# A second store buffer for one output projection, and a projection that starts three units later

## The chip, the cores and the metric

The kernel runs on one core of one Trainium2 chip. The metric is the time of one execution on the device, in microseconds (us); smaller is better. All runs quoted here are of the same state (called fast: none is over 1.5% above the fastest run of its kernel), and each kernel was timed several times beside the kernel before on the same chip.

## The reference, cut to what matters

(Condensed.) The program computes two attention blocks and all their gradients in one launch. Block A is a linear attention and takes about the first fifth of the time (its last result is copied at 217 us of 1179); the change doesn't touch it. Block B is attention with 16 query heads that share one key and one value head (2048 tokens, head size 28, padded to 32):

```python
q = (x @ wq).reshape(B, S, H, Dh).transpose(0, 2, 1, 3)
k = x @ wk
v = x @ wv
scores = einsum("bhqd,bkd->bhqk", q, k) * Dh ** -0.5
p = softmax(scores)
o = einsum("bhqk,bkd->bhqd", p, v)
return o.transpose(0, 2, 1, 3).reshape(B, S, H * Dh) @ wo     # the output projection of B
# and the gradients of this for x, wq, wk, wv, wo, from grad_out
```

The gradient of `o` begins with grad_out @ wo^T. The kernel calls that product the do-projection.

## The kernel before

The core of block B is a software pipeline of 512 units. One unit takes two 128-row key tiles for one pair of heads and 256 queries. TensorE (PE) computes scores and dP (the gradient of `p`), ScalarE (ACT) takes the exponential into `eT`, VectorE (DVE) and GpSimd (POOL) multiply to `dsT`, and PE accumulates o, dq, dk and dv. For dv the kernel needs the exponentials transposed. SyncE (SP) issues one DMA transpose for every two units, and dv uses the four transposes of a block (8 units) together, 13 units after the last one's data is ready:

```python
if u % 2 == 1:
    en = pn_.tile([P, 16, P], BF16, name="eN")                     # 12 buffers
    nc.sync.dma_start_transpose(en[:, :, :], et[...])              # 512 KB
    eN[u // 2] = en
...
if (b := due(u, 20)) is not None:
    dv_mm(b, 0)                                                    # reads eN of block b
```

Once in 64 units SyncE also loads `qX`, the queries in the layout that dk wants:

```python
if u == 14 or u % 64 == 32 and u < 448:
    qx = pq_.tile([P, 4, 2, 512], BF16, name="qX")
    for a in range(4):
        for B in range(4):                                         # 16 DMAs of 64 KB
            r0 = qc * 256 + 64 * B
            nc.sync.dma_start(qx[32 * a:32 * a + 32, B, :, :],
                              qn_d[r0:r0 + 64, :].rearrange("(j s) c -> j s c", s=2))
```

The output projection is done for two token tiles in every 64 units, four units apart, and VectorE casts each result into the one buffer, from which SyncE stores it:

```python
def out_store(u, ps):                                              # at u % 64 in (20, 24), u > 64
    i = 2 * (u // 64 - 1) + (u % 64 == 24)
    ot = flat(R3)[:, 5120:5120 + D]
    nc.vector.tensor_copy(out=ot, in_=ps[:, 0:D])                  # L636
    nc.sync.dma_start(out0[i * P:(i + 1) * P, D:2 * D], ot)        # L637
```

The do-projection is done during the first units ("the fill"), when the later stages of the pipeline have no work yet: tile `v` in unit `v + 1`, so in units 1 to 16.

## Time and profile before

| | before |
|---|---|
| time, median of 3 runs | 1177.76 us (1172.9 to 1179.81) |
| PE busy / VectorE busy / ScalarE busy | 91% / 77% / 74% |
| DMA queue 1 (SyncE's DMAs, the transposes among them), share of 16 engines | 94.3% |
| core of B, from the end of unit 1's exponentials to the end of unit 511's | 255.7 to 1097.3 us |

The page's groups of instructions (busy us, mean ns of one, then the idle time of the engine just before and what ended most of it) show VectorE idle for 44.6 us before only 16 casts, and PE idle before the score matmuls for the same cast:

```profile
L591 PE MATMUL sps<-R,R 32*128 32x256 bf16 x2048 | 248.4, 282 | 50.9 <-DVE R L636 30.9
L636 DVE CAST R<-sps 128x448 bf16<-128x448 f32 x16 | 9.9, 620 | 44.6 <-DMA out_dram<-R 42.9
```

The view of waits (who waited for whom: us in total, times, longest) has the same two, and, far down, the one wait of PE for a transpose:

```profile
DVE R L636 <- DMA out_dram<-R: 42.9, 8, 9.6
PE sps L591 <- DVE R L636: 30.9, 7, 8.9
...
PE dv_acc L591 <- DMA eN<-eT: 0.8, 1, 0.8
```

Eight pairs of casts make eight waits: the second cast of a pair may not overwrite the buffer before the first one's store has landed. The last of the eight, 7.4 us, comes after the core; 35.5 us fall in it. The timeline of VectorE (start, duration, what, idle before) at the first pair:

```profile
394.00 0.61 DVE L636 CAST R<-sps 128x448 bf16<-128x448 f32 x1
...
399.62 0.69 DVE L831 TENSOR_TENSOR dsT<-dps,eT 128x512 bf16<-128x512 f32 x1 [0.16 <-PE dps L591]
409.88 0.62 DVE L636 CAST R<-sps 128x448 bf16<-128x448 f32 x1 [9.58 <-DMA out_dram<-R]
```

Why does a store of 112 KB take from 394.6 to 409.9 us? The timeline of SyncE's queue (runs of equal DMAs are merged; x9 is nine of them) answers:

```profile
381.84 25.41 SPq L857 DMA_TRANSPOSE eN<-eT  x9
407.34 0.81 SPq L637 DMA_DIRECT2D out_dram<-R  x1
408.25 4.84 SPq L857 DMA_TRANSPOSE eN<-eT  x2
413.18 0.56 SPq L637 DMA_DIRECT2D out_dram<-R  x1
413.85 11.57 SPq L857 DMA_TRANSPOSE eN<-eT  x4
425.55 9.59 SPq L806 DMA_DIRECT2D qX<-qn_d  x16
```

SyncE issues in program order and leaves no gap, and it is behind: the cast ends at 394.6, its store goes out at 407.34. The store itself landed some 2.5 us later. I call SyncE's delay the lag: the time from the end of the exponentials that a transpose reads to that transpose's issue. It stood at 11 to 13 us here.

The view by windows (busy us and number of instructions of each engine in 25 us, then granted TensorE clock, DMA share, GB/s) shows the price. The first and second line have the stall; the third is an undisturbed stretch, in which two units take 3.04 us:

```profile
core 0: us, PE busy (x) PEld busy (x) DVE busy (x) ACT busy (x) POOL busy (x), PEclk, DMA share, GB/s
380.00:405.00 25.00, 20.69 (x362) 9.28 (x359) 19.47 (x36) 20.36 (x41) 17.60 (x20) 1.00 1.19 195
405.00:430.00 25.00, 18.88 (x314) 7.83 (x317) 18.23 (x35) 17.20 (x34) 13.69 (x16) 0.80 0.98 180
430.00:455.00 25.00, 23.81 (x438) 10.41 (x431) 23.95 (x46) 24.80 (x51) 20.70 (x24) 1.00 0.97 171
```

The granted clock (the share of TensorE's full clock that the trace records as let through) falls to 0.80 in the stretch around the stall. In the trace's record of it, it is half for 10.2 us from 406.5 us, and for 3.4 or 6.8 us at every later stall in the core. The Trainium skill, "TensorE: Matmul & The Clock Gate", section "Part 1: The HAM clock gate", has the clock halved after an idle window of about 3.4 us. The first stall fits, with PE idle for 8.9 us. But at three of the seven stalls PE's timeline has a gap of only 2.7 to 3.1 us, and the clock was halved all the same, so here a shorter idle was enough (the ends of matmuls are modelled, so such a gap is exact to some tenths of a us).

### The profile page before, as it was taken

The numbers are of one execution on the slowest core, as the hardware profiler recorded it, in microseconds if no ns is written. First come the engines' busy times: TensorE is split into PE (matmuls) and PEld (weight loads), VectorE is DVE, ScalarE is ACT, GpSimd is POOL, SyncE is SP. The second block draws the span as 40 slices with busy tenths as digits, with TensorE's granted clock in tenths as the row PEclk, the third lists the DMA queues.
The fourth block names the chain that finished last, engine by engine and source line by source line (L and its number), as shares of the span: only waits on it lengthen the run. The fifth ranks groups of instructions, "written<-read, shape, count | busy, mean of one in ns | idle before, by whom it ended". The sixth has DMA issues, their size and how long they took to land.

```text
span 1179.1 us, 38599 instructions
## 1 busy us (share of the span) xinstructions
PE 1072.2 (91%) x15379; PEld 487.1 (41%) x15388; DVE 902.6 (77%) x1733; ACT 877.4 (74%) x1724; POOL 696.6 (59%) x835
## 2 busy tenths in 40 slices
PE   7999997988999699989989997999899899989898
PEld 4555543433344244434434443444344344434344
DVE  7886400335899699989989997998899799989922
ACT  3453112356899699989989997999899799989511
POOL 9000141002778578868868885887688688768800
PEclk9999998988799899999999998999899999989999
DMA  9779798049999989999998999999899999999962
GB/s 259 126 130 185 146 172 194 24 84 214 191 166 191 188 167 185 181 189 177 188 189 160 182 185 188 169 185 183 168 183 189 187 168 180 194 177 174 244 144 75
DMA packets 684437, 202.92 MB, mean 172 GB/s; under 512 B 651232, under 2 KB 679392, under 8 KB 684256
## 3 DMA queue, kind: packets, MB, share of 16 engines
q1 hardware_dynamic: 673664, 190.26, 94.3%
q10 hardware_dynamic: 9312, 6.65, 2.0%
q0 software_dynamic: 1280, 3.55, 1.2%
q8 instruction: 120, 1.97, 0.7%
q14 instruction: 61, 0.50, 0.1%
HBM read 22.83 MB, written 15.03 MB: 32 GB/s over the span
## 4 chain that ended last, share of the span: by engine, by line
PE 59%; DVE 21%; ACT 9%; issue 4%; DMA 4%; SPq 1%; POOL 1%; ACTq 0%; DVEq 0%; POOLq 0%
PE dk_acc L591 16%; PE agen L79 10%; DVE dsT L831 8%; PE sps L591 7%; PE dps L591 6%; PE oq L591 6%; DVE dsx L894 4%; ACT eT L854 4%; PE aacc L79 4%; PE sps L79 4%; PE dv_acc L591 3%; ACT eT L826 2%; PE dps L79 2%; DVE R L840 2%; DMA out_dram<-R 2%
## 5 line engine op out<-in xcount | busy, mean ns | idle before, releaser
L834 POOL TENSOR_TENSOR dsT<-cp,eT 128x512 bf16<-128x512 bf16 x512 | 591.4, 1155 | 201.0 <-ACT cp L833 199.0
L831 DVE TENSOR_TENSOR dsT<-dps,eT 128x512 bf16<-128x512 f32 x512 | 345.8, 675 | 37.9 <-PE dps L591 29.0
L826 ACT ACTIVATE eT<-sps 128x512 bf16<-128x512 f32 x512 | 306.6, 599 | 73.3 <-PE dps L591 51.1
L894 DVE STREAM_TRANSPOSE dsx<-dsT 128x512 f32<-128x512 f32 x512 | 357.8, 699 | 2.0
L591 PEld LDWEIGHTS <-R 32*128 32x128 bf16 (+1 forms) x8192 | 200.0, 94 | 350.7 <-issue 302.9
L833 ACT ACTIVATE cp<-dps 128x512 bf16<-128x512 f32 x512 | 304.2, 594 | 14.6 <-PE dps L591 13.5
L854 ACT ACTIVATE eT<-sps 128x512 bf16<-128x512 f32 x512 | 310.6, 607 | 0.0
L591 PE MATMUL sps<-R,R 32*128 32x256 bf16 x2048 | 248.4, 282 | 50.9 <-DVE R L636 30.9
L591 PE MATMUL dk_acc<-dsx,qX 32*32 32x512 bf16 x4096 | 275.9, 385 | 0.0
L591 PE MATMUL dps<-doT,R 32*128 32x256 bf16 x2048 | 262.5, 277 | 9.5 <-DVE dsT L831 6.9
L591 PE MATMUL oq<-eT,R 128*32 128x256 bf16 x2048 | 162.2, 282 | 0.0
L591 PE MATMUL oq<-dsT,R 128*32 128x256 bf16 x2048 | 161.9, 281 | 0.1
L591 PEld LDWEIGHTS <-qX 32*32 32x32 bf16 x4096 | 81.2, 90 | 119.3 <-issue 61.3
L591 PE MATMUL dv_acc<-eN,don 128*32 128x512 bf16 x1024 | 80.7, 385 | 0.8 <-DMA eN<-eT 0.8
L521 DVE TENSOR_TENSOR osb<-R 32x512 bf16<-32x512 bf16 x4 | 1.7, 413 | 78.2 <-ACT R L518 78.2
L380 POOL MEMSET ga<- 64x448 bf16 x2 | 0.9, 469 | 90.6 <-PE agen L337 71.3
L79 PEld LDWEIGHTS <-R 128*128 128x128 bf16 (+1 forms) x416 | 34.4, 100 | 36.5 <-issue 12.6
L636 DVE CAST R<-sps 128x448 bf16<-128x448 f32 x16 | 9.9, 620 | 44.6 <-DMA out_dram<-R 42.9
L553 POOL MEMSET R<- 128x16 bf16 x1 | 0.2, 173 | 70.1 <-DVE R L552 70.1
L719 POOL TENSOR_TENSOR don<-R,rl 128x128 bf16<-128x128 bf16 x64 | 25.8, 403 | 21.2 <-DVE rl L711 21.2
L79 PE MATMUL agen<-R,R 128*128 128x448 bf16 x128 | 30.4, 369 | 3.2 <-DVE pk L227 1.9
L486 ACT ACTIVATE osb<-agen 128x448 bf16<-128x448 f32 x16 | 8.7, 542 | 28.9 <-DMA R<-xa 13.7
(203 smaller groups left out, 982.3 us busy)
## 6 DMA issues: line engine op xcount, KB each, us to landing
qX<-qn_d SPq DMA_DIRECT2D x128, 64.0 KB
out_dram<-osb ACTq DMA_DIRECT2D x44, 112.0 KB
eN<-eT SPq DMA_TRANSPOSE x256
qn_d<-dsx SPq DMA_DIRECT2D x1, 2048.0 KB
on_d<-onat SPq DMA_DIRECT2D x8, 256.0 KB
xa<-in_A_x_dram SPq DMA_DIRECT2D x8, 224.0 KB
ga<-in_grad_out_dram SPq DMA_DIRECT2D x4, 448.0 KB
xa<-in_grad_out_dram POOLq DMA_DIRECT2D x4, 448.0 KB, 5.0
```

Of the source, the lines that this page charges most:

```text
L79: nc.tensor.matmul(out_ap, lhsT=lhsT, rhs=rhs, start=start, stop=stop, tile_position=(0, 0))
L486: nc.scalar.activation(out=ot[:], in_=ps[:, :], func=ACT.Copy)
L591: nc.tensor.matmul(out, lhsT=lhsT, rhs=rhs, start=start, stop=stop, tile_position=pos, skip_group_check=True)
L636: nc.vector.tensor_copy(out=ot, in_=ps[:, 0:D])
L719: nc.gpsimd.tensor_tensor(out=dn[:], in0=dnv, in1=r_[:].to_broadcast([P, 2, 2, 32]), op=ALU.mult)
L826: nc.scalar.activation(out=et[:, u % 2, 0, :], in_=sp[0][:, :], func=ACT.Exp, scale=scale)
L831: nc.vector.tensor_tensor(out=dst[:, 0, :], in0=dp[0][:, :], in1=ew[:, w % 2, 0, :], op=ALU.mult)
L833: nc.scalar.activation(out=cp[:, :], in_=dp[1][:, :], func=ACT.Copy)
L834: nc.gpsimd.tensor_tensor(out=dst[:, 1, :], in0=cp[:, :], in1=ew[:, w % 2, 1, :], op=ALU.mult)
L840: nc.vector.tensor_scalar(out=qT_B[g][64 * hp:64 * hp + 64, qc * 256:(qc + 1) * 256], in0=oq[64:128, 0:256], scalar1=scale, scalar2=None, ...
L854: nc.scalar.activation(out=et[:, u % 2, 1, :], in_=sp[1][:, :], func=ACT.Exp, scale=scale)
L894: nc.vector.transpose(out=dsx[b][:, tp, :, :, :].rearrange("p h t c -> p (h t c)").bitcast(F32), in_=dsT[y][:, :, :].rearrange("p h c -> p ...
```

## The change

Its intent: give the second store of a pair its own buffer, so that no cast waits for a store; and start the do-projection three units later, two tiles in some units, so that it is out of the very first units and done before unit 16, from which the dP matmuls use the same two PSUM banks.

```diff
         def out_store(u, ps):
             i = 2 * (u // 64 - 1) + (u % 64 == 24)
-            ot = flat(R3)[:, 5120:5120 + D]
+            ot = pp_.tile([P, D], BF16, name="ot", bufs=1) if i % 2 else flat(R3)[:, 5120:5120 + D]
@@
-                v = u - 1
                 y = u - 18

-                if 0 <= v < NS:
-                    ps = DB[v % 2]
-                    for c in range(4):
-                        mm(ps[:, :], gbT[:, v, c, :], woTp[:, c, :], start=(c == 0), stop=(c == 3))
-                    nc.vector.tensor_copy(out=do_nat[:, v, :], in_=ps[:, :])
+                for i in range(NS):
+                    if u == 4 + 3 * i // 4:
+                        ps = DB[i % 2]
+                        for c in range(4):
+                            mm(ps[:, :], gbT[:, i, c, :], woTp[:, c, :], start=(c == 0), stop=(c == 3))
+                        nc.vector.tensor_copy(out=do_nat[:, i, :], in_=ps[:, :])
```

No work is added or removed, and the order of SyncE's DMAs is the same in both kernels.

## The prediction

> **What bounds the kernel now.** The page shows PE 91% busy, VectorE 77%, DMA queue 1 at 94.3% of 16 engines. In undisturbed stretches of the core (timeline, 440 to 480 us) two units take 3.04 us. Once in 64 units this pace breaks. The groups table has the cast of the output projection (L636) idle 42.9 us before it, 8 times, released by the store `out_dram<-R`; the waits view has PE waiting 30.9 us, 7 times, for that cast. Timeline of the first pair: the cast at 394.0 is stored only at 407.34, because SyncE issues in order and is some 13 us behind with the `eN<-eT` transposes; the second cast waits 9.58 us for that one buffer. The granted clock drops in the same stretches (windows view: 0.80 to 0.93 instead of 1.00). A semaphore wait happens on the issuing sequencer and not in the DMA engine (Trainium skill, "DMA: Bandwidth & Descriptors", section "Anatomy of one DMA — SWDGE (gpsimd) path"); the trace agrees: SyncE's rows follow one another without a gap for tens of us.
>
> **What the change does.** No work is added or removed: 16 casts (0.62 us), 16 stores, 64 matmuls of do-projection stay; SyncE's order is the same. (a) The second store of a pair gets its own buffer, so both casts have 64 units for their store: the 42.9 us of VectorE idle and the 30.9 us of PE wait go. (b) The do-projection runs in units 4 to 15 instead of 1 to 16: it leaves the half-clock start of the core (clock 0.5, 252.9 to 259.7 us; 0.53 us per matmul there, 0.26 later) and no longer shares the DB banks with unit 16. Worth 2 to 5 us of the fill.
>
> **How much is on the critical path.** Less than it looks, because the DMA stream is the next limit and almost equal. Whenever SyncE is behind, one `eN` transpose costs 2.82 to 2.88 us from issue to issue (26 of them from 334.3 to 410.5, less the other DMAs). One period of 64 units then needs 32 x 2.85 for `eN`, about 9.4 for `qX`, 2 for `on_d` and `oTq`, 1.6 for the stores: about 104 us at worst, 102 at best, against 104.3 measured (413.85 to 1039.47 over 6) and 97.3 plus two longer units for the engines. SyncE's own gaps between 400 and 1098 add to only 23 us, and its transposes get dearer when it never rests. So the stall mostly moves: PE will wait for `eN` at L591 (dv_acc), 2 to 5 us per period, shortly after `qX`, where today it waits 0.8 us in all. The fill's gain is lost at once: at 344.6 PE already waits for `eN` (chain of waits: DMA eN<-eT 339.00, 5.61 us). What remains: the first stall (9.6 us plus slow clock) is partly absorbed, 1 to 2 us in each later period, and at the end SyncE may lag 5 to 8 us instead of 0. I estimate 8 to 16 us in all.
>
> **Prediction.** 1166 us, range 1153 to 1175 (8 in 10). Chances: faster by over 2% 0.12, within 2% 0.87, slower by over 2% 0.01.
>
> **What would show it.** L636's waits for DMA gone; `dv_acc <- DMA eN` grows from 0.8 to 15 us or more; SyncE's gaps before 1090 us shrink below 8 us; transposes start more than 8 us after their exp nearly throughout; the last core exp ends some 10 us earlier; the clock still dips about once a period.
>
> **What would make it wrong.** If a saturated transpose costs 2.75 us or less, or the DMA lag never reaches the 13 us at which PE has to wait, the gain goes to 25 to 35 us (faster by over 2%). If the loads after unit 512, queued behind late transposes, delay the tail, the gain goes to nearly zero.

## The result

| | before | after |
|---|---|---|
| time, median of 4 runs each | 1177.78 us | 1164.24 us (1161.1 to 1166.75) |
| ratio of the fast runs | | 0.9897 (95%: 0.9858 to 0.9936) |
| VectorE's wait at the cast for a store | 42.9 us, 8 times | none |
| PE's wait for `eN` | 0.8 us | 16.6 us, 9 times |
| gaps over 0.2 us between SyncE's DMAs, first to last transpose | 24.1 us | 2.9 us |
| lag of SyncE, mean over the transposes | 6.5 us | 11.1 us |
| core of B, unit 1 to unit 511 | 841.6 us | 826.6 us |

Ratios, here and below, are of fast runs timed in the same rounds, so not quite the ratio of the medians. The kernel is 1.0% faster. (Of the 42.9 us, the 7.4 us after the core stay as idle time: there the same cast now waits 7.0 us for PE. The two profiled executions differ by more, 1179.1 against 1159.4 us of span, because the core also began 6.4 us earlier in the second; the code before it is the same, and over all runs its start moves between 249 and 256 us.)

The casts after, in VectorE's timeline: the second one finds its own buffer free and follows 6.8 us after the first.

```profile
388.55 0.61 DVE L636 CAST R<-sps 128x448 bf16<-128x448 f32 x1
...
395.31 0.63 DVE L636 CAST ot<-sps 128x448 bf16<-128x448 f32 x1 [0.46 <-ACT cp L833]
```

SyncE's queue after. Nothing about it has changed, except that it never rests:

```profile
377.56 22.36 SPq L857 DMA_TRANSPOSE eN<-eT  x8
400.02 0.97 SPq L637 DMA_DIRECT2D out_dram<-R  x1
401.09 5.34 SPq L857 DMA_TRANSPOSE eN<-eT  x2
406.52 0.71 SPq L637 DMA_DIRECT2D out_dram<-ot  x1
407.33 11.57 SPq L857 DMA_TRANSPOSE eN<-eT  x4
419.02 9.98 SPq L806 DMA_DIRECT2D qX<-qn_d  x16
429.12 21.25 SPq L857 DMA_TRANSPOSE eN<-eT  x8
```

After `qX` the lag is 18.8 us, and the dv matmuls of the next block find their transposes missing. PE's timeline:

```profile
438.31 0.38 PE L591 MATMUL dv_acc<-eN,don 128*32 128x512 bf16 x2
439.40 0.38 PE L591 MATMUL dv_acc<-eN,don 128*32 128x512 bf16 x1 [0.71 <-DMA eN<-eT]
443.06 1.01 PE L591 MATMUL dv_acc<-eN,don 128*32 128x512 bf16 x5 [3.28 <-DMA eN<-eT]
```

The wait that was 0.8 us in all is now this line of the view of waits, while no line there has the cast wait for a store:

```profile
PE dv_acc L591 <- DMA eN<-eT: 16.6, 9, 4.1
```

In the windows, the stretch with the two stores is whole now, and the next one, which was undisturbed before, has lost 5 us of ScalarE's work and a little of its clock:

```profile
405.00:430.00 25.00, 23.69 (x436) 10.53 (x430) 23.86 (x46) 24.60 (x50) 20.26 (x23) 1.00 0.98 162
430.00:455.00 25.00, 20.16 (x342) 8.11 (x341) 18.68 (x35) 19.25 (x39) 15.78 (x17) 0.93 1.19 188
455.00:480.00 25.00, 23.52 (x435) 10.35 (x428) 23.76 (x46) 24.52 (x49) 20.48 (x24) 1.00 1.19 194
```

So the stall has moved by some 40 us and become smaller. The period of 64 units went from 104.2 to 103.25 us (from unit 89 to unit 473), where the engines alone take 99.4 (the kernel `after_skip8` below).

### The profile page after: what moved, and what is told of

It reads as the page before. It is cut to its first block, busy times and chain, and to the rows that moved or that the text cites. A ratio compares the mean times of both kernels' runs of the same rounds, so it can differ in the third digit from the quotient of the medians.

```text
span 1159.4 us, 38606 instructions
## 1 busy us (share of the span) xinstructions
PE 1070.2 (92%) x15388; PEld 485.6 (42%) x15388; DVE 902.6 (78%) x1733; ACT 876.8 (76%) x1724; POOL 696.4 (60%) x835
## 3 DMA queue, kind: packets, MB, share of 16 engines
q8 instruction: 120, 1.97, 0.7%
## 4 chain that ended last, share of the span: by engine, by line
PE 59%; DVE 21%; ACT 8%; DMA 4%; issue 4%; SPq 2%; POOL 1%; ACTq 0%; DVEq 0%; POOLq 0%
PE dk_acc L591 16%; PE agen L79 10%; DVE dsT L831 8%; PE sps L591 7%; PE dps L591 6%; PE oq L591 6%; DVE dsx L894 5%; PE sps L79 4%; ACT eT L854 4%; PE dv_acc L591 3%; PE aacc L79 3%; DMA eN<-eT 3%; ACT eT L826 3%; PE dps L79 2%; DVE R L840 2%
## 5 line engine op out<-in xcount | busy, mean ns | idle before, releaser
L591 PE MATMUL dv_acc<-eN,don 128*32 128x512 bf16 x1024 | 85.0, 387 | 16.6 <-DMA eN<-eT 16.6
L591 PEld LDWEIGHTS <-don 128*32 128x32 bf16 x1024 | 28.7, 98 | 21.2 <-issue 20.4
```

The costliest lines, as they stand in the source:

```text
L591: nc.tensor.matmul(out, lhsT=lhsT, rhs=rhs, start=start, stop=stop, tile_position=pos, skip_group_check=True)
```

## The experiments

The theory: (1) the gain is all from the second buffer; (2) the cast waited because of the store's place in SyncE's queue, not because of the transfer; (3) what is left over is the length of that queue of DMAs, so about half of PE's stall came back as waits for `eN`; (4) the moved do-projection is worth nothing. The rivals: the fill gives part of the gain; a store takes too long for one buffer in any case; what is left after the change is the pace of the engines. Eight kernels were run, each with three rounds.

For most of them the table has how long the profiled execution took from the last exponential of one unit to that of another, in us. It shows where a kernel gains or loses, free of when the core began:

| units | before | after | buf_only | shift_only | before_pool | after_qx4 | before_qx4 | buf_qx4 |
|---|---|---|---|---|---|---|---|---|
| 1 to 17 | 30.7 | 32.5 | 30.3 | 32.4 | 30.6 | 31.8 | 29.8 | 30.4 |
| 17 to 53 | 60.8 | 59.9 | 62.2 | 60.0 | 60.6 | 59.8 | 59.8 | 59.9 |
| 53 to 87 | 52.5 | 52.5 | 53.8 | 52.5 | 52.5 | 52.5 | 52.5 | 52.5 |
| 87 to 481 | 651.7 | 635.6 | 636.1 | 648.7 | 640.8 | 613.5 | 622.0 | 613.2 |
| 481 to 511 | 45.9 | 46.0 | 45.9 | 46.1 | 45.9 | 46.1 | 45.9 | 45.9 |
| SyncE's lag, mean | 6.5 | 11.1 | 11.0 | 6.1 | 11.7 | 4.8 | 3.3 | 9.1 |

### buf_only: the second buffer alone

The edit to the kernel before is the first hunk of the change, without the second.

> Only the second store buffer; the do-projection stays in units 1 to 16. Theory (the stall at the cast is all of the gain): 1161 to 1167 us, the same as with both parts, PE waits about 15 us for eN at dv_acc. Rival (part of the gain is in the fill): 1168 to 1174 us.

Measured: 1164.73 us, ratio to before 0.9917 (0.9876 to 0.9957). PE waited 19.3 us for `eN`. To within the noise that is the whole gain of the change, as the theory expected.

### shift_only: the do-projection alone

The edit is the second hunk, without the first.

> Only the do-projection moved; one store buffer. Theory: no gain, 1175 to 1181 us, the cast still waits some 40 us for its store, because PE is held to the eN transposes by unit 52 whatever the fill does. Rival (the fill gains): 1170 to 1174 us.

Measured: 1175.22 us, ratio 1.0029 (0.9964 to 1.0093). The cast still waited 37.9 us for its store. The rival is refuted: the moved do-projection gains nothing that can be measured. The table says how. With the do-projection in units 4 to 15 the first 16 units of the table take about 32 us instead of about 30, and the next 36 take somewhat less: to unit 53 it is 92.4 us here, 91.5 in before and 92.5 with the buffer alone.

The clock goes with it. The prediction had the do-projection leave the slow start of the core. But that slow start got longer. The two windows, first of before and then of after, cover 10 us that lie alike to the start of the core (unit 1 ended at 255.7 and at 249.3 us). In them VectorE casts three do-projection tiles before and one after:

```profile
253.00:263.00 10.00, 8.55 (x48) 2.71 (x50) 2.08 (x3) 5.99 (x11) 0.00 (x0) 0.66 1.02 189
```

```profile
247.00:257.00 10.00, 8.21 (x41) 2.77 (x42) 0.69 (x1) 5.57 (x11) 0.00 (x0) 0.56 1.05 196
```

The granted clock is 0.66 in the first and 0.56 in the second. In the clock record of the one profiled execution of each of the ten kernels, the half clock at the start of the core lasts 10.2 us in the five kernels with the moved do-projection, and 3.4 or 6.8 us in the five without it. That the emptier units 1 to 3 are what keeps the clock low is argued from this, not shown by itself.

### before_pool: one buffer, the store issued by GpSimd

```diff
-            nc.sync.dma_start(out0[i * P:(i + 1) * P, D:2 * D], ot)
+            nc.gpsimd.dma_start(out0[i * P:(i + 1) * P, D:2 * D], ot)
```

> Kernel before, one buffer, but GpSimd issues the 16 stores, so that a store doesn't stand behind SyncE's late transposes. Theory (the wait is the place in the queue, not the transfer): the wait of the cast for DMA falls from 43 us to under 10 us and the time to 1160 to 1168 us, as with two buffers. Rival (one buffer is too few because a store takes longer than four units, 6 us): the wait stays above 25 us and the time above 1173 us.

Measured: 1165.6 us, ratio 0.9918 (0.986 to 0.9976). VectorE waits only 0.7 us, once, for a store, with one buffer. PE waits 20.5 us for `eN` instead:

```profile
PE dv_acc L591 <- DMA eN<-eT: 20.5, 13, 4.1
```

So four units are time enough for a store that is issued at once; it was the place in SyncE's queue that cost. And this kernel stops at the same 1165 us as the two buffers, though it cures the stall in another way. That points at a common next limit.

### after_qx4: the load of qX in 4 DMAs

```diff
                     for a in range(4):
-                        for B in range(4):
-                            r0 = qc * 256 + 64 * B
-                            nc.sync.dma_start(qx[32 * a:32 * a + 32, B, :, :],
-                                              qn_d[r0:r0 + 64, :].rearrange("(j s) c -> j s c", s=2))
+                        nc.sync.dma_start(qx[32 * a:32 * a + 32, :, :, :],
+                                          qn_d[qc * 256:(qc + 1) * 256, :].rearrange("(B j s) c -> j B s c", B=4, s=2))
```

> Changed kernel, with the qX load of 64 units in 4 DMAs of 256 KB instead of 16 of 64 KB; same bytes. Theory (the DMA stream that SyncE issues is now the limit): SyncE's 9.4 us for qX fall to 4 to 6 us, PE's 16.6 us of waits for eN fall to under 5 us, and the time falls by 10 to 25 us to 1140 to 1155 us. Rival (what is left is the pace of the engines): within 4 us of 1164.

Measured: 1139.37 us (1136.9 to 1147.25), ratio to before 0.9714 (0.9662 to 0.9765). This beats both kernels. In SyncE's timeline (this kernel's lines are two lower than those of before) the load takes 1.97 us where it took 9.98:

```profile
402.58 11.79 SPq L855 DMA_TRANSPOSE eN<-eT  x4
414.47 1.97 SPq L804 DMA_DIRECT2D qX<-qn_d  x4
416.54 35.38 SPq L855 DMA_TRANSPOSE eN<-eT  x11
```

No wait for `eN` is left in the view of waits, the clock has no dip between unit 32 and unit 511, and the window that lost 5 us in the changed kernel is full:

```profile
430.00:455.00 25.00, 23.80 (x438) 10.40 (x431) 23.89 (x46) 24.80 (x51) 20.37 (x23) 1.00 1.20 192
```

The rival "what is left is the pace of the engines" is refuted, since the engines do the same work and the core takes 803.7 us instead of 826.6. SyncE's time for the load alone got shorter than the 4 to 6 us that I expected, 2.4 us in the mean over the eight loads. But part of its cost moved: the first transpose behind each load now takes SyncE 4.9 us in the mean, where it took 1.9 in the changed kernel. Load and follower together take 7.3 us instead of 10.9, and SyncE still never rests here (2.4 us of gaps).

### before_qx4: one buffer, but SyncE keeps up better

The same edit in the kernel before.

> One store buffer, do-projection in units 1 to 16, but qX in 4 DMAs. Theory (the stall at the cast is SyncE's lag, and qX is its largest source): the lag at the store falls from 5 to 13 us to about 4 us, the cast waits under 15 us for its store instead of 43, time 1138 to 1150 us; so the two buffers are worth under 8 us once SyncE keeps up. Rival (one buffer costs its stall whatever the lag): the cast waits 30 us or more and the time is 1160 us or more.

Measured: 1144.42 us, ratio 0.9737 (0.968 to 0.9795). The cast waited 15.0 us, in 3 of 8 pairs (just over, not under, the 15 that I gave), and one of those waits, of 7.4 us, came after the core, as in the kernel before; in the core it is 7.6 us against 35.5:

```profile
DVE R L636 <- DMA out_dram<-R: 15.0, 3, 7.4
PE sps L591 <- DVE R L636: 7.8, 5, 4.1
```

One buffer is nearly enough when SyncE is only 3 us behind. The second buffer, which was worth 10 to 13 us at the long lag, is worth about 6 here (1144.42 against 1138.22, next run; the two ranges overlap).

### buf_qx4: two buffers and the short load, do-projection not moved

> Two store buffers and qX in 4 DMAs, do-projection left in units 1 to 16. Theory (the shifted do-projection gives back between units 16 and 52 what it costs before): within 4 us of the run with the shift, 1136 to 1143 us. Rival (the shift was worth something and the DMA stream hid it): 1143 us or more.

Measured: 1138.22 us (1135.21 to 1142.07), ratio 0.9691 (0.9642 to 0.974). It is the fastest of all medians, but 1.2 us from the run with the shift is within the spread. Even with the shorter queue the moved do-projection gains nothing. The theory in the expectation, that the shift gives back by unit 52 what it costs before, does not show here: to unit 53 the kernel with the shift (`after_qx4`) takes 91.6 us by the table, and this one 90.3. Nor is the DMA limit far away: SyncE never rests (2.4 us of gaps), its lag grows from 7 us in the first 64 units to 12 us in the last but one, and PE waits for `eN` twice, 0.8 us in all.

### after_skip8: one transpose in eight left out

```diff
+                        if u // 2 % 8 == 7:
+                            eN[u // 2] = en          # the one before, again: dv is wrong
+                        else:
                             en = pn_.tile([P, 16, P], BF16, name="eN")
                             nc.sync.dma_start_transpose(...)
```

> Changed kernel, wrong on purpose (dv alone): every 8th eN transpose is left out and the eN before it used again, so the DMA stream has 32 transposes fewer; all engine work stays. Theory: PE's waits for eN vanish and the time is that of the engines' pace, 1133 to 1143 us, as with qX in 4 DMAs. Rival (the qX edit helped by something else than the stream's length): above 1150 us.

Measured: 1139.98 us, ratio 0.972 (0.9657 to 0.9782). Its output is wrong, which doesn't matter for the time. No wait for `eN` is left, and SyncE now has 96.1 us of gaps between its DMAs. With that much slack, and with qX left in 16 DMAs, the core takes 802.8 us: as in the run with the short load (803.7). Two unlike ways to shorten the queue end at the same time, and 96 us of slack in the queue gain nothing beyond it, so this is the pace of the engines.

### after_qx32: the load of qX in 32 DMAs of 32 KB

```diff
-                        for B in range(4):
-                            r0 = qc * 256 + 64 * B
-                            nc.sync.dma_start(qx[32 * a:32 * a + 32, B, :, :],
-                                              qn_d[r0:r0 + 64, :].rearrange("(j s) c -> j s c", s=2))
+                        for B in range(8):
+                            r0 = qc * 256 + 32 * B
+                            nc.sync.dma_start(qx[32 * a + 16 * (B % 2):32 * a + 16 * (B % 2) + 16, B // 2, :, :],
+                                              qn_d[r0:r0 + 32, :].rearrange("(j s) c -> j s c", s=2))
```

> Changed kernel with qX in 32 DMAs of 32 KB, the same bytes. Theory (SyncE's stream is the limit and a DMA's issue costs it 0.52 us whatever the size): 16 more issues add about 8 us in each of six to seven periods, so 1205 to 1225 us, nearly all of it as PE waiting for eN. Rival (bytes are what counts, or the stream has slack): within 8 us of 1164.

Measured: 1230.67 us, ratio to before 1.0473 (1.0417 to 1.053). The direction and the kind are as the theory has it; the size is a miss, 6 us above the range. The load takes 17.39 us, and there are eight loads, not six to seven, which I had miscounted: SyncE's time for `qX` grew from 66.4 us in all to 127.8, by 61.4 us, and the kernel by 66. The waits, too, are not of one kind only; ScalarE waits as well, for `eT` buffers that late transposes still read:

```profile
PE dv_acc L591 <- DMA eN<-eT: 64.0, 30, 6.0
ACT eT L826 <- DMA eN<-eT: 26.8, 7, 6.5
```

```profile
326.70 17.39 SPq L806 DMA_DIRECT2D qX<-qn_d  x32
```

In this state the kernel lengthens by about a microsecond for each microsecond that its stream of DMAs lengthens. In the same way the 16 DMAs of 64 KB cost about 8 to 10 us per load, and making them 4 took 25 us off the changed kernel. SyncE's time for `qX` shrank by 48 us (66.4 to 18.0), but some 24 of these came back in the eight transposes behind the loads (4.9 us each instead of 1.9).

## Why the prediction was right, point by point

- **The time.** 1166 us was predicted and 1164.24 measured; the class, within 2%, was given 0.87.
- **The stall and its cause.** The cast's 42.9 us of waits for the store went to none, and the run with GpSimd's store shows that SyncE's lag made the wait.
- **The next limit.** The prediction put a saturated transpose at 2.82 to 2.88 us from issue to issue. Where transposes follow one another with over 3 us of lag, the mean is 2.86 us before and 2.82 after. It put the period at 102 to 104 us; it is 103.25. It expected PE to wait 15 us or more for `eN`, 2 to 5 us per period shortly after `qX`; it waits 16.6 us, 1.1 to 4.1 us in each of six periods, the first time 4.0 us at unit 116. It put the lag at which PE has to wait at 13 us; all these waits come at blocks whose last transpose lags by 14.0 to 17.9 us. SyncE's gaps were to fall below 8 us, and fell to 2.9. This is why an obstacle of 31 us of PE's waits was worth 13 us (30.9 + 0.8 us of waits before, 16.6 after: 15.1 us less, and the core is 15.0 us shorter): the same stream of DMAs that made the store late also makes the transposes late.
- **The lag.** "More than 8 us nearly throughout" holds for 216 of 256 transposes. At the end of the core it is 4.3 us, not 5 to 8. That SyncE itself does the waiting, for which the prediction cites the skill, is shown less by rows without a gap than by the gaps: in the kernel before, 24 of the 27 gaps over 0.2 us in front of a transpose end within 0.03 us of the end of the exponentials that it reads.
- **The last exponential.** It was to come some 10 us earlier. It came 21.4 us earlier, of which 6.4 are the earlier start; the core is 15 us shorter. After the core both profiled executions take about as long, 81.8 and 83.5 us.
- **The clock.** It was to dip about once a period. In fact four dips of 3.4 us are left in the core, where seven of 3.4 to 10.2 us were before (a half-clock stretch of 20.5 us in the fill, from about 285 us, is in both and not counted). The waits for `eN` come in shorter pieces (at most 4.1 us; PE waited up to 8.9 us for the cast before).
- **What was wrong: the fill.** "It leaves the half-clock start of the core … Worth 2 to 5 us of the fill" failed. The moved do-projection makes the half-clock start longer (10.2 us in every kernel that has it, 3.4 or 6.8 us in every one that hasn't), and the first 16 units are about 2 us slower. The prediction then said that the fill's gain would be lost at unit 52 to the transposes. There was no gain to lose, and the runs with the short load show none either. The time came out right in spite of this, because the prediction gave the fill no weight in its sum.

What stays open is what in the path of a transpose takes the 2.8 to 2.9 us, SyncE's issue or the DMA engines' movement. With `qX` in 4 DMAs a transpose costs 2.97 us in the mean where SyncE is behind, because the first one after each load is dearer (4.9 us against 1.9); that the load's bytes are what it waits for is likely, but the runs don't separate the two further. Why the moved do-projection lengthens the half clock stays open too.

## What to carry to other kernels

When an engine waits for a buffer whose store is late, look at the issuing queue before adding a buffer: here the store stood behind 13 us of other DMAs because the queue itself was near its limit, and the second buffer moved about half of the wait to the next user of that queue. Count the queue's time per period (issues times their cost) and compare it with the engines' period; here 103 against under 100 us told the result. The better edit was to shorten the queue: a quarter of the DMAs for the same bytes was worth more (30 us alone) than the second buffer (10 us alone), and made most of the latter needless.

## What the Trainium skill lacked or had wrong

- "DMA: Bandwidth & Descriptors", section "Issuing engines are not separate DMA queues", says that the sequencer's time to initiate a DMA is usually small relative to the DMA. For many small loads behind one another it set the length: each of 16 DMAs of 64 KB took 0.52 us of SyncE, 8 to 11 us a load, and the same bytes in 4 DMAs took 1.8 to 3.5 us (and 3 us more on the transpose behind them); in 32 DMAs, 16 to 19 us. How long one such DMA takes to land is not in the trace.
- The same page, section "Latency and other measured facts", gives 261 GB/s for a DMA transpose with a non-contiguous middle dimension and about 350 to 400 for the contiguous case. Here a transpose of 128 x 2048 bf16 (512 KB) within SBUF, issued back to back, took about 2.85 us, which is 184 GB/s by that size; whether the issue or the movement sets this is open.
- No page that I read has what a saturated stream does to the issuing sequencer: in the kernel before, the issue of one transpose took SyncE 2.4 us in the mean (1.3 to 3.6) where it was under 1 us behind, and 2.7 us in the mean where it was over 3 us behind; an ordinary store waits behind them (12.7 us in the first pair).
- "TensorE: Matmul & The Clock Gate", section "Part 1: The HAM clock gate", has the clock halved after an idle window of about 3.4 us. Here it was halved at PE gaps of 2.7 to 3.1 us (three stalls of the kernel before), and in `before_qx4` at one of 2.2 us. The half-clock stretches here last 3.4, 6.8, 10.2, 13.7, 17.1 or 20.5 us, multiples of its window. The page doesn't say that moving early matmuls to a later point can lengthen the slow start (10.2 us against 3.4 to 6.8 here).
